# Attention front end of a fused kernel: transposes of F split, V projections ahead of P V, third g block in y's bank, finer weight slices

## Chip, cores, metric

One core of a Trainium2 chip. The metric is device microseconds of one execution, median over runs. The kernel before takes 568.84 us here (568.69 to 569.04, 4 runs).

## The reference, cut to what matters

```python
# attention with keys and values projected from 1024 to 64 rows, 8 batches x 8 heads, head size 64
k_proj = einsum('ks,bhsd->bhkd', E, k);  v_proj = einsum('ks,bhsd->bhkd', F, v)
attn   = softmax(q @ k_proj^T / 8);      x = attn @ v_proj          # -> x [8192, 512]
# gated feed-forward
out = (silu(x @ w_gate) * (x @ w_val)) @ w_out                      # 512 -> 1536 -> 512
```

The kernel cuts the 8192 tokens into 16 chunks of 512 and the 1536 hidden columns into 12 "features" of 128. For each chunk and feature there is a **g block** and a **v block** of four 128x128x512 matmuls. In the first chunk the first two features are done in half blocks of 256 tokens, as parts of x become ready.

## The kernel before

The change touches only what runs before the steady loop. The attention of the first chunk is done in four parts 0 to 3 (two head groups by two token halves): `u_S` scores and exp, `u_R` row sums, `u_N` normalization (on GpSimd; that of part 3 on DVE), `u_A` transposes of the normalized P, `u_PV*` P V product and its copy into xT, the feed-forward's input. Before and between them stand **warm-up matmuls** (`warm(n)`): n products of zeros whose result nobody reads.

```python
def u_V0(p0, p1, at):            # V projection of head pairs p0..p1, block diagonal in one bank
    t = bank(at, [P, p1 - p0, P], FP32, "kvp")
    nc.tensor.matmul(out=t, lhsT=zeros, rhs=zeros, start=True, stop=False)
    for j in range(NJ):
        for c in range(2):       # 16 matmuls; in the trace the two of a pair start 3 ns apart
            nc.tensor.matmul(out=t[64*c:64*c+64, :, 64*c:64*c+64], lhsT=FT[:, j, :], ...)
    nc.scalar.copy(out=BDV[0][:, p0:p1, :], in_=t[:])

def f_mm(c, f, w, i=None):       # one (half) block of g (w=0) or v (w=1)
    if i != 1:
        half[c, f, w] = bank("gv"[w], [P, CW], FP32, "gv"[w] + "ps")
    ...                          # four matmuls over wg or wv
# ... (cut) order of the front end in the kernel before, from part 3's scores on:
        u_S(0, 3, "v"); u_R(0, 3); u_A(0, 0, act); u_N(0, 3, dve)
        u_V0(0, 2, "y");  u_PV2(0, 0, 0, 0, act)
        u_V0(2, 3, "y");  u_A(0, 2, act)
        u_V0(3, 4, "v");  u_PV1(0, 0, 2, 0, dve)
        u_A(0, 1, dve);   u_PV1(0, 0, 3, 0, act)
        u_A(0, 3, act)
        load_w_gv(2, 4, (1,))
        f_mm(0, 0, 0, 0); u_PV2(0, 0, 0, 1, dve)
        f_mm(0, 0, 1, 0); f_mm(0, 1, 0, 0)
        u_PV2(0, 0, 1, 1, act); f_mm(0, 1, 1, 0)
```

The first dma calls of GpSimd are, in order: q, k, q, F, v (three parts), then g's weights of feature 0, v's of feature 0, g's of feature 1, v's of feature 1, and so on. `load_w_gv(c0, c1, which)` loads features c0 to c1 of g (0), v (1) or both.

The softmax here doesn't subtract the row's maximum and nothing guards it: scores larger than these inputs give would overflow.

## Time and profile before

| | before |
|---|---|
| time | 568.84 us |
| TensorE busy | 560.2 of 566.9 us |
| TensorE's waits for other engines, whole run | 3.0 us in 5 waits |
| first half block of the feed-forward starts | 20.70 us |
| third v block starts (dense from there on) | 25.93 us |

How to read it: TensorE is the bound from end to end, so a change to the front end can shift only the moment at which the dense stretch begins, as long as no later wait takes the lead back. That moment is the start of the third v block; the prediction shows the lines.

### The profile page before, as it was taken

Reading aid. Unit: us, or ns where it says so; the run is one execution under the profiler, and the core shown is the slowest. Engines: PE = TensorE matmul, PEld = TensorE weight load, DVE = VectorE, ACT = ScalarE, POOL = GpSimd, SP = SyncE. Lnnn points to the kernel's source line nnn. Section 1 sums busy time; section 2 is a strip of 40 time slices with the busy share of each in tenths; the row PEclk is TensorE's granted clock in tenths of the full one; section 3 lists DMA queues with packets and bytes.
Section 4 is the critical chain, followed back from the end, with each engine's and each line's share of the span. In section 5 each row is a group of like instructions: output and inputs, shape, how many; then the busy total and the mean of one; then the engine's idle time right before and its main releaser. Section 6 shows DMA issues by size and latency. Waiting matters only on the chain.

```text
span 566.9 us, 7938 instructions
## 1 busy us (share of the span) xinstructions
PE 560.2 (99%) x2970; PEld 266.3 (47%) x2970; DVE 339.2 (60%) x576; ACT 236.0 (42%) x417; POOL 110.4 (19%) x124
## 2 busy tenths in 40 slices
PE   8999999999999999999999999999999999999997
PEld 4654444444444444444444444444444444444444
DVE  3786664766476645766466655666547665545550
ACT  3664352444435433443434434354343543443222
POOL 6851250124012400124002230023100220000000
PEclk9999999999999999999999999999999999999999
DMA  9999989729913795029940499105990214100012
GB/s 201 194 200 188 175 126 199 141 57 187 192 50 74 113 196 119 38 57 163 183 83 37 76 185 204 38 19 101 200 183 20 57 38 75 38 37 32 25 38 93
DMA packets 111159, 62.78 MB, mean 111 GB/s; under 512 B 64272, under 2 KB 102416, under 8 KB 111120
## 3 DMA queue, kind: packets, MB, share of 16 engines
q0 software_dynamic: 42896, 29.49, 36.1%
q1 hardware_dynamic: 67392, 31.46, 26.2%
q10 hardware_dynamic: 832, 1.31, 0.8%
q8 instruction: 23, 0.38, 0.3%
q14 instruction: 16, 0.13, 0.1%
HBM read 60.29 MB, written 16.78 MB: 136 GB/s over the span
## 4 chain that ended last, share of the span: by engine, by line
PE 97%; ACT 1%; DVE 1%; issue 0%
PE gps L377 29%; PE yps L415 29%; PE vps L377 29%; PE kvp L150 3%; PE sc L271 2%; PE pv L328 2%; PE warm L513 1%; ACT ee L275 0%; ACT AT L138 0%; DVE BD L138 0%; ACT th L389 0%; PE qTp L237 0%; PE efp L501 0%; PE aTp L317 0%; PE pv L343 0%
## 5 line engine op out<-in xcount | busy, mean ns | idle before, releaser
L396 DVE SCALAR_TENSOR_TENSOR s<-th,gps 128x512 f32<-128x512 f32 x192 | 130.3, 679 | 134.4 <-ACT th L389 134.0
L377 PE MATMUL gps<-xT,wg 128*128 128x512 bf16 (+1 forms) x776 | 197.6, 377 | 0.1
L377 PE MATMUL vps<-xT,wv 128*128 128x512 bf16 (+1 forms) x776 | 197.5, 377 | 0.0
L415 PE MATMUL yps<-wo,hT 128*128 128x512 bf16 (+1 forms) x780 | 194.5, 376 | 0.0
L389 ACT ACTIVATE th<-gps 128x512 f32<-128x512 f32 x192 | 114.6, 597 | 159.0 <-PE gps L377 153.9
L401 DVE TENSOR_TENSOR hT<-s,vps 128x512 bf16<-128x512 f32 x192 | 131.9, 687 | 20.4 <-DVE s L396 0.5
L301 POOL TENSOR_TENSOR AAd<-ee,rr 128x512 bf16<-128x512 f32 x56 | 58.2, 1041 | 342.5 <-issue 180.6
L415 PEld LDWEIGHTS <-hT 128*128 128x128 bf16 x780 | 76.2, 98 | 89.9
L377 PEld LDWEIGHTS <-wv 128*128 128x128 bf16 x776 | 74.0, 98 | 83.3 <-issue 2.9
L377 PEld LDWEIGHTS <-wg 128*128 128x128 bf16 x776 | 74.0, 98 | 81.3 <-issue 1.2
L425 ACT ACTIVATE ysb<-yps 128x512 f32<-128x512 f32 (+1 forms) x65 | 38.4, 590 | 77.7 <-PE yps L415 77.7
L138 ACT CAST xT<-pv 128x512 bf16<-128x512 f32 (+1 forms) x62 | 35.9, 581 | 52.5 <-PE pv L328 50.3
L286 DVE TENSOR_REDUCE zz<-ee 128x8 f32<-128x512 f32 x64 | 43.4, 679 | 22.1 <-ACT ee L275 22.1
L275 ACT ACTIVATE ee<-sc 128x512 f32<-128x512 f32 x64 | 38.2, 597 | 19.8 <-PE sc L271 18.7
L271 PEld LDWEIGHTS <-qTd 128*128 128x128 bf16 x224 | 17.2, 98 | 13.2 <-DMA qTd<-qb 0.2
L328 PE MATMUL pv<-AT,BDV 128*128 128x512 bf16 x60 | 22.4, 379 | 0.1
L271 PE MATMUL sc<-BD,qTd 128*128 128x128 bf16 x224 | 21.6, 219 | 0.0
L288 DVE RECIPROCAL rr<-zz 128x8 f32<-128x8 f32 x64 | 13.0, 203 | 6.6 <-DVE zz L286 0.5
L108 POOL DMA_DIRECT2D qb<-in_q_dram x18 | 16.3, 907 | 1.4 <-POOLq L651 0.8
L150 PE MATMUL kvp<-kb,ET 128*64 128x512 bf16 (+1 forms) x72 | 15.5, 358 | 0.0
L162 DVE CAST BDV<-kvp 64x256 bf16<-64x256 f32 x7 | 3.0, 426 | 20.0 <-ACT ks L158 17.8
L150 PE MATMUL kvp<-vb,FT 128*64 128x512 bf16 x56 | 13.4, 382 | 0.0
(66 smaller groups left out, 137.6 us busy)
## 6 DMA issues: line engine op xcount, KB each, us to landing
out_dram<-ysb SPq DMA_DIRECT2D x63, 256.0 KB, 2.3
qb<-in_q_dram POOLq DMA_DIRECT2D x14, 512.0 KB, 18.1
kb<-in_k_dram POOLq DMA_DIRECT2D x7, 1024.0 KB, 11.0
vb<-in_v_dram POOLq DMA_DIRECT2D x7, 1024.0 KB, 14.5
wo<-in_moe_w_out_dram POOLq DMA_DIRECT2D x2, 768.0 KB, 21.9
wg<-in_moe_w_gate_dram POOLq DMA_DIRECT2D x5, 256.0 KB, 8.4
wv<-in_moe_w_val_dram POOLq DMA_DIRECT2D x5, 256.0 KB, 9.0
kraw<-in_k_dram ACTq DMA_DIRECT2D x2, 512.0 KB, 4.9
```

The costliest lines, as they stand in the source:

```text
L138: (nc.scalar.copy if eng is nc.scalar else eng.tensor_copy)(out=out, in_=in_)
L150: nc.tensor.matmul(out=t[lo : lo + 64, h0:h1].rearrange("p h d -> p (h d)"), lhsT=w[:, j, :], rhs=src[b][:, h0:h1, j, :], start=(j == 0), ...
L271: nc.tensor.matmul(out=ps[:, n, :], lhsT=t[:, n, :], rhs=BD[b % 2][:, 4 * g + n, :], start=True, stop=True)
L275: nc.scalar.activation(out=e[:].rearrange("p h j k -> p (h j k)"), in_=ps[:].rearrange("p a k -> p (a k)"), func=AF.Exp, scale=scale,)
L286: nc.vector.reduce_sum(out=z[:], in_=e[:], axis=AX.X)
L301: eng.tensor_tensor(out=a.rearrange("p j h k -> p h j k"), in0=ee.pop((b, u))[:], in1=rr.pop((b, u))[:].unsqueeze(3).to_broadcast([P, 4, 2 ...
L377: nc.tensor.matmul(out=ps[:, ts], lhsT=(wg, wv)[w][:, kt, f * P : (f + 1) * P], rhs=x[:, kt, ts], start=(kt == 0), stop=(kt == NKT - 1),)
L389: nc.scalar.activation(out=th[:], in_=ps[:], func=AF.Tanh, scale=0.5)
L396: nc.vector.scalar_tensor_tensor(out=s1[:], in0=th[:], scalar=1.0, in1=g[:], op0=ALU.add, op1=ALU.mult)
L401: nc.vector.tensor_tensor(out=hT[c][:, f, :], in0=s1[:], in1=ps[:], op=ALU.mult)
L415: nc.tensor.matmul(out=yy[c][:, cs], lhsT=hT[c][:, f, i * P : (i + 1) * P], rhs=wo[:, f, cs], start=(f == 0), stop=(f == NFT - 1),)
L425: nc.scalar.activation(out=ysb[:, cs], in_=yy[c][:, cs], func=AF.Copy, scale=0.5)
```

## The change

Its intent: start the feed-forward earlier. F is transposed earlier and its copies are shared between DVE and ACT; V of the first two head pairs is projected in a wide form (8 matmuls instead of 17); the first g half block stands ahead of the transposes of P parts 1 and 3; the third g block borrows y's bank; the normalization of part 3 moves from DVE to GpSimd; the weights come in slices of 1, 1, 1, 2, 2, 2, 2, 1 features.

```diff
+    def u_V0w(p0, p1, at):          # 8 matmuls of 256 columns into partitions 64..127, two ACT copies
...
-            half[c, f, w] = bank("gv"[w], [P, CW], FP32, "gv"[w] + "ps")
+            where = "y" if (c, f, w) == (0, 2, 0) else "gv"[w]
+            half[c, f, w] = bank(where, [P, CW], FP32, where + "ps")
...
-        load_w_gv(2, 4, (0,))
+        load_w_gv(2, 3)
...
-        warm(1)
+        turn(1, "a", (0,), dve)
...
+        turn(1, "a", (1,))
         u_S(0, 2, "g")
...
-        turn(1, "a", (0,))
+        load_w_gv(3, 5, (0,))
...
-        turn(1, "a", (1,))
         u_S(0, 3, "v")
         u_R(0, 3)
+        u_N(0, 3)
+        load_w_gv(3, 5, (1,))
         u_A(0, 0, act)
-        u_N(0, 3, dve)
-        u_V0(0, 2, "y")
+        u_V0w(0, 2, "y")
+        u_V0(2, 3, "v")
         u_PV2(0, 0, 0, 0, act)
-        u_V0(2, 3, "y")
-        u_A(0, 2, act)
-        u_V0(3, 4, "v")
+        u_A(0, 2, dve)
+        u_V0(3, 4, "y")
         u_PV1(0, 0, 2, 0, dve)
+        u_PV1(0, 0, 3, 0, act)
+        f_mm(0, 0, 0, 0)
         u_A(0, 1, dve)
-        u_PV1(0, 0, 3, 0, act)
+        f_mm(0, 0, 1, 0)
+        u_PV2(0, 0, 0, 1, dve)
         u_A(0, 3, act)
-        load_w_gv(2, 4, (1,))
-        f_mm(0, 0, 0, 0)
-        u_PV2(0, 0, 0, 1, dve)
-        f_mm(0, 0, 1, 0)
         f_mm(0, 1, 0, 0)
         u_PV2(0, 0, 1, 1, act)
         f_mm(0, 1, 1, 0)
...                                  # later slices: (5,7), q, q, (7,9), (9,11), (11,12)
```

More of the change, by code (lines that the diff above doesn't have):

```diff
@@ L185, in u_V0 @@
         nc.scalar.copy(out=BDV[0][:, p0:p1, :], in_=t[:])
+    def u_V0w(p0, p1, at):
+        t = bank(at, [P, p1 - p0, 2, D], FP32, "kvp")
+        for j in range(NJ):
+            nc.tensor.matmul(
+                out=t[64:P].rearrange("p a c d -> p (a c) d"),
+                lhsT=FT[:, j, :],
+                rhs=vb[0][:, 2 * p0 : 2 * p1, j, :],
+                start=(j == 0),
+                stop=(j == NJ - 1),
+            )
+        for c in range(2):
+            rows = slice(64 * c, 64 * c + 64)
+            nc.scalar.copy(out=BDV[0][rows, p0:p1, rows], in_=t[64:P, :, c, :])
     def u_KT(b, at="a", prs=(0, NPAIR)):
@@ L495, with turn @@
         nc.vector.memset(ks[0][64:P], 0.0)
-        def turn(which, at, halves=(0, 1)):
+        nc.vector.memset(BDV[0][:, 0:2], 0.0)
+        def turn(which, at, halves=(0, 1), eng=nc.scalar):
             for half in halves:
@@ L506, in turn @@
                 js = slice(4 * half, 4 * half + 4)
-                copy(nc.scalar, (ET, FT)[which][:, js, :], ps[:])
+                copy(eng, (ET, FT)[which][:, js, :], ps[:])
         def warm(n):
@@ L581 @@
         nc.vector.memset(BDV[1][:], 0.0)
-        load_w_gv(4, 6)
+        load_w_gv(5, 7)
         load_q(0, 1, hs=(0, 4))
-        load_w_gv(6, 8)
         load_q(0, 1, hs=(4, 8))
-        load_w_gv(8, 10)
-        load_w_gv(10, 12)
+        load_w_gv(7, 9)
+        load_w_gv(9, 11)
+        load_w_gv(11, 12)
         load_q(1, 0)
```

## The prediction

> **What bounds the kernel now.** I read four views, in this order: the page, who waited for whom on TensorE, the timeline of TensorE over the first 75 us, and the landing times of single transfers. The page first. Columns of its first line: busy us, share of the span, number of instructions.
>
> ```profile
> PE 560.2 (99%) x2970; PEld 266.3 (47%) x2970; DVE 339.2 (60%) x576; ACT 236.0 (42%) x417; POOL 110.4 (19%) x124
> PE   8999999999999999999999999999999999999997
> PEclk9999999999999999999999999999999999999999
> ```
>
> TensorE is busy from end to end at the full clock. Nothing in the diff touches a tile after feature 2 of the first chunk of tokens except the order of loads, so all gain and all loss lie in the first 25 us or so. The waits of TensorE in the whole run (us in total, times, longest) say how little can be had there:
>
> ```profile
> PE sc L271 <- DVE BD L138: 0.7, 1, 0.7
> PE pv L343 <- ACT BDV L185: 0.7, 1, 0.7
> PE pv L355 <- ACT AT L138: 0.2, 1, 0.2
> PE aTp L317 <- DVE xT L138: 0.2, 1, 0.2
> ```
>
> The last three, 1.1 us, are in the stretch that is rearranged. The timeline (start us, duration us, what; L377 is the feed-forward, L178 the V projection, L343 the P V product, L317 a transpose of P) shows where that stretch ends:
>
> ```profile
> 17.88 0.39 PE L343 MATMUL pv<-AT,BDV 128*128 128x256 bf16 x2 [0.68 <-ACT BDV L185]
> ...
> 20.48 0.38 PE L317 MATMUL aTp<-ident_bf,AA 128*128 128x128 bf16 x4 [0.18 <-DVE xT L138]
> 20.70 0.60 PE L377 MATMUL gps<-xT,wg 128*128 128x256 bf16 x4
> ...
> 21.36 0.60 PE L377 MATMUL vps<-xT,wv 128*128 128x256 bf16 x4
> ...
> 22.45 0.60 PE L377 MATMUL vps<-xT,wv 128*128 128x256 bf16 x4
> 22.89 0.78 PE L377 MATMUL gps<-xT,wg 128*128 128x256 bf16 x4
> 23.50 0.60 PE L377 MATMUL vps<-xT,wv 128*128 128x256 bf16 x4
> ...
> 25.07 1.02 PE L377 MATMUL gps<-xT,wg 128*128 128x512 bf16 x4
> 25.93 1.03 PE L377 MATMUL vps<-xT,wv 128*128 128x512 bf16 x4
> ```
>
> The starts tell what the durations hide. A half block of four 256-column matmuls is followed 0.44 us later by the next, a whole block of 512 columns 0.86 us later. Two starts are late: after 22.89 comes 23.50 (0.61, so 0.17 lost: that block waits midway for the last xT, which ACT finishes at 23.24), and the last half block at 24.38 is followed at 25.07 and not at 24.82 (0.25 lost: the third g waits for a g bank, which DVE frees at 25.02). From 25.93 on the starts are dense, 0.86 us apart, with 0.45 us of gaps in all up to 75 us. So **the number to predict is the start of the third v block (feature 2), 25.93 us**; whatever that moves by, the end moves by.
>
> The landings matter because the weights come just in time. The first half of v's weights for feature 0, issued at 8.65, has this line:
>
> ```profile
> DMA to landing us min/median/max: 12.5/12.5/12.5
> ```
>
> It lands at 21.18, 0.18 us before its use at 21.36. Read the same way: g of feature 0 lands at 18.84, g of feature 1 at 21.36 (used 21.80), v of feature 1 at 21.95 (used 22.45), the pair 2-3 at 23.29 and 24.65.
>
> **What the Trainium skill says.** "PSUM — Partial Sum Buffer", Specifications, gives 8 banks per partition; the pools take 2 (g), 2 (v), 1 (y) and 3 (attention), so the third g can only wait or borrow y's. The trace agrees (the 0.25 us). "DMA: Bandwidth & Descriptors", section Why a DMA increments its semaphore by 16 and not by 1: all 16 engines post one and only the full count means landed. The trace shows what that costs: of the sixteen increments for v of feature 0, fifteen came by 19.58 and the last at 21.18. "Runtime: NRT & Kernel Launch", Terms: instruction memory is refilled in 16 KiB blocks. In the trace's packets a 16,384-byte one of the instruction queue starts at 19.15 and holds one DMA engine for 0.945 us; that is the late sixteenth. "GPSIMD Engine Reference", Engine selection, calls a two-input elementwise operation on GpSimd some 2 times slower than on VectorE; here it does not hold: the normalization took 1.04 us on POOL and 1.13 on DVE.
>
> **The change part by part.** I replayed the new order by hand, with durations from this trace and about 0.04 to 0.1 us from one engine's end to the next one's start.
>
> *F's turns.* F lands at 13.11; its first four transposes (0.44 us) take the place of one warm matmul (0.39 us), whose time was a wait for ks (ACT, to 13.57) anyway. Cost 0. One FT copy goes to DVE, the other stays on ACT but ahead of the exps. Exp 0.60 and FT copy 0.38 had alternated (starts 14.94, 15.68, 16.42); now the exps follow each other at 0.49: about 15.01, 15.50, 15.99. The last exp is 0.43 us earlier, and with it the copy of the first transposed P (16.91 to 16.48).
>
> *V ahead.* The wide form does 8 matmuls of 256 columns (0.109 each, 0.87 us) for 16 of 128 that ran two at a time (0.42 us from first to last start) and a zeroing: TensorE about 0.25 us more, while it waits anyway. Its result is ready at 16.9, two copies of some 0.27 end at 17.5; V of pair 2, gated by its data (16.88), fills TensorE until about 17.15. The first P V starts at 17.55 instead of 17.88. The transposes of P part 2 follow at 17.85 (18.63 before), V of pair 3 at 18.2 (data 18.11), the two small P V products at 18.7 and 19.0, and the copies of xT end at 19.7. The first g half block then starts at 19.1, waits for these copies, and ends about 19.9: **some 1.2 us earlier than before** (21.14).
>
> *What follows it.* The order is now transposes of P part 1 (20.1), v of feature 0, P V, transposes of part 3, g of feature 1, P V, v of feature 1, then the second halves. Part 3 is normalized on POOL behind two weight issues (0.75 each): ready near 20.6. From the transposes of part 3 a chain runs that TensorE cannot cover: to ACT's copy 0.42, copy 0.59, P V, 0.42 to its copy, 0.59, the second half of a g block. From the start of v's half block of feature 0 to the v block that stood at 23.50 this makes 0.65 + 1.07 + 1.06 + 0.22, about 3.0 us; before, the transposes of part 3 came ahead of everything. So that block starts at (landing of v of feature 0) + 3.06. **Break-even is a landing at 20.45.** If the data is there at 20.1, the P V ahead of it waits for DVE's copy and the block starts at 23.35: gain 0.15.
>
> *Third g in y's bank.* It removes the 0.25 us, but the v block behind needs v's first bank, freed by tanh 0.60, DVE 0.69 and 0.69: about 2.37 us after the block of 23.50, where it was 2.43. Gain 0.06, not 0.25.
>
> *Slices.* Same bytes. The stretch of small slices moved 178 to 186 GB/s against 196 in the two-feature ones, so four more small transfers of 128 KB cost 4 x 0.05 = 0.2 us of queue. With them feature 3 lands at about 24.7 (g) and 26.05 (v), its uses stand at 26.80 and 27.66; the second chunk's q lands at 30.05 and 31.4, uses 31.98 and 34.37; the last w_out at 57.3, use 59.41. All hidden.
>
> Sum if v of feature 0 is early: -0.15 - 0.06 = -0.2 us. If it lands at 21.18 as now: 21.18 + 3.06 = 24.24 against 23.50, +0.74 - 0.06 = +0.7 us.
>
> **Rivals.** *(1) The instruction fetch moves behind the transfer.* TensorE's stream is about 20 instructions shorter up to here, so the same instruction count is reached later in the work; if the fetch starts after 19.3, v of feature 0 lands at 19.6 and the time is 568.7. *(2) The fetch stays or comes slightly earlier*, since TensorE reaches that work sooner: the landing stays between 20.3 and 21.2, TensorE idles up to 1.1 us at the first v half block and the time is 568.9 to 569.6. For it: no load ahead of that transfer changes. *(3) The gain of 1.2 us at the first g carries through*: 567.7. Against it: g and v of feature 1 land at 21.36 and 21.95, which caps the start of the second halves near 22.5 instead of 22.89 even if all else is free. *(4) A later wait eats it all*: POOL now makes parts 1 and 3 between weight issues; were it 1 us later than I have it, 569.5. The trace speaks against, since no issue there would wait for a semaphore.
>
> **Range and chances.** I give the early landing (568.7) somewhat over half, the late one (569.3 to 569.6) a third, the rest to (3). The centre is 568.8. The range 568.1 to 569.7 spans all but the far ends. Two per cent is 11.4 us, ten times the whole of TensorE's waits here: same is all but certain.
>
> **What would show it.** Right: first P V near 17.55, first g half block done near 19.9, no wait before the third g, later starts dense from the third v block. The deciding reading is the start of the first v half block and what ended the wait before it: a landing of wv before 20.5 means a gain of 0.1 to 0.2, one near 21.2 a loss. Wrong: a third v block before 25.3, or a new wait for weights after 26 us.

## The result, and the profile after

568.57 us (568.5 to 568.64, 4 runs) against 568.84 us; ratio 0.9995, 95% interval 0.9978 to 1.0012. Ratios here are the mean time of one kernel's fast runs over that of the other's of the same rounds, so not quite the ratio of the medians quoted.

TensorE's line of the page, and its waits (us in total, times, longest), of the changed kernel:

```profile
PE 560.3 (99%) x2960; PEld 266.2 (47%) x2960; DVE 339.2 (60%) x578; ACT 235.7 (42%) x416; POOL 113.0 (20%) x127
```

```profile
PE sc L286 <- DVE BD L138: 0.7, 1, 0.7
PE efp L520 <- DMA Eraw<-in_E_dram: 0.4, 1, 0.4
PE pv L358 <- ACT BDV L200: 0.3, 1, 0.3
PE pv L358 <- ACT AT L138: 0.2, 1, 0.2
```

The wait for the first P V is down from 0.7 to 0.3 us, the one ahead of the last transposes is gone, and the 0.2 us for ACT's copy of transposes (`AT`) now stand in front of the last P V product, in the middle of the feed-forward's half blocks. The wait for E lies ahead of all edited work on TensorE. The timeline of TensorE in the changed kernel, same stretch (L395 feed-forward, L358 P V, L332 transposes):

```profile
17.68 0.39 PE L358 MATMUL pv<-AT,BDV 128*128 128x256 bf16 x2 [0.26 <-ACT BDV L200]
...
19.20 0.89 PE L395 MATMUL gps<-xT,wg 128*128 128x256 bf16 x4
...
20.16 0.60 PE L395 MATMUL vps<-xT,wv 128*128 128x256 bf16 x4
20.83 0.38 PE L358 MATMUL pv<-AT,BDV 128*128 128x256 bf16 x2
21.05 0.39 PE L332 MATMUL aTp<-ident_bf,AA 128*128 128x128 bf16 x4
...
22.11 0.38 PE L358 MATMUL pv<-AT,BDV 128*128 128x256 bf16 x2 [0.24 <-ACT AT L138]
...
23.38 0.60 PE L395 MATMUL vps<-xT,wv 128*128 128x256 bf16 x4
...
24.69 1.03 PE L395 MATMUL yps<-xT,wg 128*128 128x512 bf16 x4
25.74 1.02 PE L395 MATMUL vps<-xT,wv 128*128 128x512 bf16 x4
```

The first g half block starts 1.5 us earlier (20.70 to 19.20) and the first v half block 1.2 us (21.36 to 20.16), but the v block that stood at 23.50 stands at 23.38 and the third v at 25.74 instead of 25.93. The gain shrinks between 20.83 and 23.38: transposes of part 3 at 21.05, their copy on ACT (21.47 to 22.06), P V at 22.11, its copy (22.52 to 23.11), second half of the g block. That is the chain that the prediction named. And 0.07 of the 0.19 us are not the change's: the first scores, ahead of any edited instruction but one memset in DVE's idle time, already start at 10.83 instead of 10.90. Such a shift differs from run to run: in the two later profiles of the same kernel they start at 10.62 and 10.60. v of feature 0 landed early (issued at 8.55; at 19.47):

```profile
DMA to landing us min/median/max: 10.9/10.9/10.9
```

### The profile page after: what moved, and what is told of

Read it like the earlier page. It is cut to its first block, busy times and chain, and to the rows that moved or that the text cites. A ratio compares the mean times of both kernels' runs of the same rounds, so it can differ in the third digit from the quotient of the medians.

```text
span 566.8 us, 7925 instructions
## 1 busy us (share of the span) xinstructions
PE 560.3 (99%) x2960; PEld 266.2 (47%) x2960; DVE 339.2 (60%) x578; ACT 235.7 (42%) x416; POOL 113.0 (20%) x127
## 4 chain that ended last, share of the span: by engine, by line
PE 97%; ACT 1%; DMA 1%; DVE 0%; issue 0%; POOL 0%
PE yps L433 29%; PE vps L395 29%; PE gps L395 29%; PE kvp L150 3%; PE sc L286 2%; PE pv L343 2%; DMA Eraw<-in_E_dram 1%; ACT ee L290 0%; PE qTp L252 0%; PE aTp L332 0%; PE warm L532 0%; PE efp L520 0%; PE pv L358 0%; ACT AT L138 0%; POOL AA L316 0%
## 5 line engine op out<-in xcount | busy, mean ns | idle before, releaser
L395 PE MATMUL vps<-xT,wv 128*128 128x512 bf16 (+1 forms) x776 | 197.5, 377 | 0.0
L395 PE MATMUL gps<-xT,wg 128*128 128x512 bf16 (+1 forms) x772 | 196.9, 377 | 0.0
L395 PEld LDWEIGHTS <-wv 128*128 128x128 bf16 x776 | 73.9, 98 | 83.5 <-issue 3.2
L395 PEld LDWEIGHTS <-wg 128*128 128x128 bf16 x776 | 74.0, 98 | 80.9 <-issue 0.8
```

Source lines behind the costliest of these rows:

```text
L395: nc.tensor.matmul(out=ps[:, ts], lhsT=(wg, wv)[w][:, kt, f * P : (f + 1) * P], rhs=x[:, kt, ts], start=(kt == 0), stop=(kt == NKT - 1),)
```

## The experiments

All times are against the kernel before on the same chip (568.73 to 568.77 us median in each set). "Early" and "late" below mean the landing of feature 0's v weights. The landing is known only for the one profiled run of each set; the others are called early or late by their times. Each interval is some 0.25% (1.4 us) wide, so differences of a few tenths rest on single profiles and on how runs group.

### 1. The changed kernel again, twice

No edit. 

> The changed kernel as it is, for a closer interval and a second profile. Theory A (the change works by an earlier first feed-forward block; what it gains is bounded by the chain from the transposes of P part 3, and 0.07 of the 0.19 us seen at the third v block were there before the change begins to act, at the first scores): 0.1 to 0.3 us under the kernel before, third v block at 25.7 to 25.8. Rival B (the landing of the first v weights is luck: this profile caught it early at 19.47 us, others catch it late at 21.2): some runs or this profile show the third v block at 26.4 or later and times near 569.3.

Measured: 569.10, 569.14, 569.29, 569.18 and 568.48 us; ratio 1.0005 (0.9992 to 1.0017). **Four of the five are slower than the kernel before.** The profile, of the run with 569.10, shows why (landing of v of feature 0; below it TensorE's timeline):

```profile
DMA to landing us min/median/max: 12.3/12.3/12.3
```

```profile
20.94 0.61 PE L395 MATMUL vps<-xT,wv 128*128 128x256 bf16 x4 [0.83 <-DMA wv<-in_moe_w_val_dram]
...
23.94 0.60 PE L395 MATMUL vps<-xT,wv 128*128 128x256 bf16 x4
...
26.30 1.02 PE L395 MATMUL vps<-xT,wv 128*128 128x512 bf16 x4
```

Issued at 8.55, the weights landed at 20.90 (fifteen of sixteen increments by 19.30). The v block behind the chain stands at 23.94 = 20.90 + 3.04; the third v at 26.30. Rival B of the expectation holds: the same program has early and late runs.

The last set had the changed kernel once more. 

> The changed kernel once more, on the chip of the three runs above: a mixture of early runs (568.4 to 568.7) and late ones (569.1 to 569.3); in the profile, fetch after the first increment of v of feature 0 and landing near 19.5, or fetch before it and landing near 20.9.

Measured: 569.05, 568.50, 568.57, 568.67, 568.46; ratio 0.9998 (0.9985 to 1.0010). The profiled run is the late one: landing 20.86, third v 26.26. Over the 14 runs of the changed kernel nine are early, by their times, with a mean of 568.55 us and five late with a mean of 569.15; together 568.77, which is what the kernel before takes. The four runs of the first result were all early.

### 2. The third g in g's own bank

```diff
-            where = "y" if (c, f, w) == (0, 2, 0) else "gv"[w]
+            where = "gv"[w]
```

> The changed kernel with the third g block in g's own bank again. Theory A: the third v block behind it waits for v's bank anyway, so only about 0.06 us is lost: third g late by 0.2 to 0.25, third v at 25.80 to 25.85, time 0.05 to 0.1 us above the changed kernel. Rival C (borrowing y's bank is what gained the 0.27 us): 0.2 to 0.3 us above the changed kernel, third v near 26.0.

Measured: 568.63, 568.60, 568.55, 568.48 and a late 569.17 us. The early mean, 568.57, is that of the changed kernel. Timeline:

```profile
23.40 0.60 PE L395 MATMUL vps<-xT,wv 128*128 128x256 bf16 x4
...
24.97 1.02 PE L395 MATMUL gps<-xT,wg 128*128 128x512 bf16 x4
25.84 1.03 PE L395 MATMUL vps<-xT,wv 128*128 128x512 bf16 x4
```

The third g is 0.26 us later behind the block at 23.40, the third v only 0.08 (2.44 against 2.36). Here the third v follows the third g directly (0.87 us); in the changed kernel it starts 1.05 us behind it, 0.19 us more than the 0.86 of two dense blocks, as v's bank is not free yet. So all but 0.08 us of the early third g is lost again. Rival C falls.

### 3. Feature 0's v weights late on purpose

```diff
-        load_w_gv(0, 1)
+        load_w_gv(0, 1, (0,))
         load_w_gv(1, 2, (0,))
+        load_w_gv(0, 1, (1,))
```

> The changed kernel with feature 0's v weights loaded behind feature 1's g weights, so that they land late on purpose (about 21.2 where 19.47 was). Theory A: the transposes of P part 3 stand behind the first v half block, so everything moves: first v half block at about 21.2, the v block that stood at 23.38 at landing + 3.06 = 24.2, third v at 26.6, time 0.8 to 0.9 us above the changed kernel. Rival D (the later weights set the pace, feature 1's land late anyway): the third v block moves by less than 0.3 us.

Measured: 569.37 us (569.30 to 569.39), 0.8 above the early runs of the changed kernel. Landing 21.18, first v half block 21.22, then:

```profile
24.22 0.60 PE L395 MATMUL vps<-xT,wv 128*128 128x256 bf16 x4
```

24.22 = 21.18 + 3.04, third v 26.58. Rival D falls. One landing makes the difference, and with it always late there are no early runs.

### 4. More instructions ahead

```diff
-            for _ in range(n):   # each rhs=zeros[:] (512 columns)
+            for _ in range(2 * n):   # each rhs=zeros[:, 0:256]
```

> The changed kernel with every warm-up matmul of 512 columns cut in two of 256: same time on TensorE, 17 more matmuls (34 more instructions) ahead of everything. Theory A: the fetch of 16,384 bytes at 19.12 us is TensorE's instruction stream and comes at an instruction count, so it comes earlier, at 17.5 to 18.7 us, and holds one of the sixteen increments of the first g or v weights: v of feature 0 complete at 19.9 to 21.2 instead of 19.47, third v block 0 to 0.8 us later. Rival E (the fetch comes at a time, or belongs to another engine): fetch at 19.1 as now and no change in landings or time.

Measured: 569.64 us (569.49 to 570.65). The 16,384-byte packet starts at 17.03 instead of 19.12. The DMA view counts it, between 19 and 20 us in the changed kernel and between 17 and 18 us here (queue, kind, packets, MB, share of 16 engines):

```profile
q8 instruction: 1, 0.02, 5.9%
```

```profile
q8 instruction: 1, 0.02, 5.6%
```

It now holds the last part of the raw v, whose last increment comes at 19.21, 1.2 us behind the fifteenth (17.98):

```profile
19.25 0.44 PE L178 MATMUL kvp<-vb,FT 128*64 128x64 bf16 x16 [0.84 <-DMA vb<-in_v_dram]
```

The third v stands at 26.70. So the packet is moved by TensorE's instruction stream, not bound to a moment, and the transfer that ends while it is moved lands late. So do those behind it: the last increments of g and v of feature 0 came at 19.66 and 20.40, 0.96 and 0.97 us behind their fifteenth. The expectation had named these two as what would bind; it was the raw v, and the loss at the third v (0.96 us) is above the 0 to 0.8 expected. One of the five runs, 570.65, stands alone; its granted clock was 0.997, that of the others 0.999 or 1.0.

### 5. The slices of before

The changed kernel with the loads of before: `load_w_gv(2, 4, (0,))` in place of `(2, 3)`, `load_w_gv(2, 4, (1,))` behind the three normalizations, then (4,6), q, (6,8), q, (8,10), (10,12).

> The changed kernel with the weight slices and the order of loads of the kernel before. Theory A: the new slices are hidden, so this changes nothing by itself: early runs at 568.5 to 568.6, late ones at 569.1 to 569.3, third g and v at the same distance (1.31 and 2.36 us) behind the v block of the second halves of feature 0. Rival F (the single slice of feature 2 lands just in time and is part of the gain): a wait for wg or wv before the third g or v block, third v later by over 0.2 us.

Measured: 568.52 us (568.50 to 568.91); third v at 25.73. No effect on the time, as theory A has it. But there is a hidden one: in this kernel, which has no weight issue between the three normalizations, the transfers fall to some 160 GB/s between 22 and 26 us, and the transposed q of batch 1 lands at 60.52 instead of 59.75. Its first use stands at 61.00, so 0.5 us of slack hid it. The next runs met it.

### 6. Part 3 first, and the whole chain early

First run: both weight issues behind the three normalizations, and

```diff
         u_A(0, 1, dve)
+        u_A(0, 3, act)
         f_mm(0, 0, 1, 0)
         u_PV2(0, 0, 0, 1, dve)
-        u_A(0, 3, act)
-        f_mm(0, 1, 0, 0)
         u_PV2(0, 0, 1, 1, act)
+        f_mm(0, 1, 0, 0)
         f_mm(0, 1, 1, 0)
```

> The changed kernel with the two normalizations of parts 1 and 3 on GpSimd ahead of the weight issue between them, and the transposes of part 3 ahead of the first v half block, both P V products behind it. Theory A (the chain from these transposes sets the second halves): where v of feature 0 lands early (19.5), the v block that stood at 23.38 starts near 22.8, the third v at 25.1 and the time is near 568.0; where it lands late (20.9), the third v stands near 25.5 and the time is near 568.3. Rival D (the landing of feature 1's weights, 21.2 and 21.5, sets the second halves): gain under 0.2 us, 568.4 or more.

Measured: 567.91 to 569.81, median 568.40 (6 runs). The profiled run is late (landing 20.93, 568.66 us): block behind the chain at 23.16 and third v at 25.52, where the changed kernel's late run has 23.94 and 26.30:

```profile
23.16 0.60 PE L395 MATMUL vps<-xT,wv 128*128 128x256 bf16 x4
...
25.52 1.02 PE L395 MATMUL vps<-xT,wv 128*128 128x512 bf16 x4
```

So the chain from part 3's transposes is what sets these starts, and rival D falls at the third v. But only 0.4 us of the 0.8 reach the end. The six runs do not form two groups, and the longest, 569.81 us at a granted clock of 1.0, is not explained.

Second run: as the first; besides, `u_A(0, 1)` between the two small P V products, `u_A(0, 3)` right behind the first g half block, the P V product of part 1 ahead of the first v half block, and the third v in a bank of the attention pool (`"ya"[w] if (c, f) == (0, 2)`).

> As the run with part 3 first, and the transposes of part 1 between the two small P V products, those of part 3 right behind the first g half block, and the third v block in a bank of the attention pool besides the third g in y's. Theory A: v block of the second halves of feature 0 near 22.55, third v directly behind third g, near 24.75, and about 567.6 in early runs; 25.3 and 568.2 in late ones. If the third v still waits (for DVE, not for a bank) or for its weights, the gain over the run with part 3 first is under 0.15 us.

Measured: 568.52 us median (567.74 to 568.66). Third v at 24.92, 0.8 us ahead of the changed kernel, in an early run, but the time of that run, 568.52, is the changed kernel's. Where it went (timeline, TensorE's waits for transfers after 26 us):

```profile
35.33 1.04 PE L395 MATMUL vps<-xT,wv 128*128 128x512 bf16 x4 [0.28 <-DMA wv<-in_moe_w_val_dram]
...
60.98 0.40 PE L286 MATMUL sc<-BD,qTd 128*128 128x128 bf16 x4 [0.24 <-DMA qTd<-qb]
```

It hit two landings that had been hidden: v's weights of feature 7 took 0.4 us of the lead, the transposed q of batch 1 (60.93) the rest; the scores start at 60.98, in the changed kernel at 61.00. The transfers themselves were slower. Stretches of 2 us, last column GB/s; first this run, then the changed kernel:

```profile
24.00:26.00 2.00, 1.95 (x12) 0.93 (x11) 1.79 (x4) 1.01 (x2) 2.00 (x4) 1.00 1.30 155
26.00:28.00 2.00, 2.00 (x11) 0.94 (x10) 1.90 (x4) 0.60 (x1) 1.23 (x2) 1.00 1.35 170
```

```profile
24.00:26.00 2.00, 1.98 (x14) 1.14 (x13) 1.69 (x3) 1.02 (x3) 2.00 (x4) 1.00 1.40 187
26.00:28.00 2.00, 2.00 (x11) 0.92 (x10) 1.79 (x4) 0.69 (x2) 2.00 (x3) 1.00 1.44 195
```

All three kernels with 3.8 us or more between two starts of weight issue (this one, the one before it, experiment 5) show it; the kernel before, with 3.6 us, and the changed one, with 2.8, do not or hardly; single 512-byte packets, 60 ns as a rule, then took up to 1.2 us (experiment 5). The length of that pause was never changed alone: the slices, their order and the place of the issue changed with it. So that the pause slows the transfers is a guess from these profiles, and what a packet waits for was not tested.

### 7. TensorE's order alone

The loads and GpSimd's order as in the changed kernel; only

```diff
-            where = "y" if (c, f, w) == (0, 2, 0) else "gv"[w]
+            where = "ya"[w] if (c, f) == (0, 2) else "gv"[w]
...
         u_A(0, 1, dve)
+        u_A(0, 3, act)
         f_mm(0, 0, 1, 0)
         u_PV2(0, 0, 0, 1, dve)
-        u_A(0, 3, act)
```

> The changed kernel with the loads and GpSimd's order as they are; only TensorE's order and a bank differ: the transposes of part 3 stand ahead of the first v half block, and the third v block borrows a bank of the attention pool. What the two runs before it gained at the third v block (0.7 to 0.8 us) they lost by 61 us, where the transposed q of the second batch lands at 60.9 to 61.1 instead of 59.75, because the weight issue held back behind GpSimd's normalizations let the transfers fall to 140 to 177 GB/s between 22 and 28 us. Theory A with this addition: transfers as in the changed kernel, transposed q at 59.6 to 59.8, third v at 25.1 to 25.2 where v of feature 0 lands early and 25.5 where late; 567.9 to 568.1 in early runs, 568.2 to 568.4 in late ones. If the gain is lost again with the transposed q at 59.75, another wait behind 26 us takes it.

Measured: 568.20 us (568.04 to 568.43); ratio to the kernel before 0.9990 (0.9977 to 1.0002). In the profiled run, an early one (568.04):

```profile
20.46 0.40 PE L332 MATMUL aTp<-ident_bf,AA 128*128 128x128 bf16 x4 [0.34 <-POOL AA L316]
20.70 0.60 PE L395 MATMUL vps<-xT,wv 128*128 128x256 bf16 x4
...
24.37 1.03 PE L395 MATMUL gps<-xT,wg 128*128 128x512 bf16 x4
25.23 1.03 PE L395 MATMUL vps<-xT,wv 128*128 128x512 bf16 x4
```

The third v follows the third g without a gap, now that it has a bank of its own, and stands 0.51 us ahead of the changed kernel's early run; the end, too, comes 0.51 us earlier (566.26 against 566.77), and the transposed q lands at 59.44. Of the 0.51 us 0.2 are an early start (first P V at 17.48 instead of 17.68). Counted from the first P V, the v block of feature 0's second halves comes 0.12 us sooner (5.58 against 5.70 us) and the third v 0.31 us (7.75 against 8.06): in an early run the borrowed bank brings 0.19 us and the moved transposes 0.12, since these now wait 0.34 us for GpSimd's normalization of part 3. The mean of the five runs, 568.21, is 0.34 under the changed kernel's early ones. No run is above 568.43, as expected if late data finds the transposes that start the chain already done; no late run was profiled here, so that is not shown. By the mean this is the best version, ahead of both kernels in every one of its five runs but by one part in a thousand, and its interval against the kernel before just includes 1.

### 8. Moving the fetch later: three misses

Changed kernel without the last three warm-up matmuls: 

> The changed kernel without its last three warm-up matmuls (the single one and the pair), which stand in waits: TensorE reaches every later instruction 6 instructions sooner in count, so by theory A the fetch of its instruction stream comes 0.2 to 0.6 us later than 18.9 to 19.1, behind the last of v of feature 0's packets; all five runs then are early, 568.4 to 568.6. Rival B' (early or late is decided by something else, as the moment of the first loads): both kinds of runs again, with the fetch where it was. If the clock falls[...], the record of the clock shows it and the run says nothing.

Measured: 569.00, 569.03, 569.07, 568.38, 568.22 us; in the profile, a late one, fetch at 18.75, landing 20.83. Both kinds of runs again; a miss.

Changed kernel with the second warm-up group cut from 4 to 1 (`warm(4)` to `warm(1)`): 

> The changed kernel with the second group of warm-up matmuls cut from 4 to 1. The run that dropped three later ones (at 9.7 and 11.5 us) did not move the fetch later; the one that added 34 instructions before 8 us moved it 2.1 us earlier. If what starts the fetch is an instruction count reached before 9.7 us, 6 instructions fewer at 7 to 8 us move it 0.2 to 0.6 us later, to 19.2 to 19.7, behind v of feature 0's packets (first increment 18.9 to 19.1): all runs early, 568.4 to 568.7. If the fetch does not follow the count: 18.7 to 19.15 again and both kinds of runs, as before.

Measured: 568.98 to 569.31 us, all late; fetch at 18.73, landing 20.76. A miss: against the changed kernel's late profiles (fetch at 18.87 and 18.78, first feed-forward block at 19.00 and 18.97) fetch and block (18.93) have hardly moved, and not later. That all five are late is not explained.

That edit with the order of experiment 7: 

> Both edits together. If both hold: all runs early, third v near 25.15, 567.9 to 568.1, better than the kernel before by 0.7 us.

Measured: 568.12 to 568.18 in four runs and 569.15 in one; fetch at 19.01, landing 19.51, third v at 25.33. The fetch edit adds nothing to experiment 7. The one long run was not profiled: a late landing alone should have cost less, by experiment 7's expectation. Its granted clock was 0.997, that of the other four 1.0; 0.3% of the span is up to 1.7 us, so the clock may well be the cause.

## Why the prediction was right, point by point

- **Bound and place.** Right: TensorE's busy time is 560.3 us (560.2 before), and beyond the third v block the starts are dense in both kernels.
- **F's turns and V ahead.** Right in mechanism, by the timeline; no run undid either part alone. First P V at 17.68, predicted 17.55. The mis-sized term is the start of ACT's two copies of V: taken as 16.97, they started at 17.09 (ACT was copying P's transposes until 17.07) and ended at 17.63, not 17.5. Behind the first g half block the next work starts at 19.94, predicted 19.9.
- **Chain of 3.06 us behind the landing of v of feature 0.** Right, and the best tested step: 3.04 in experiments 1 and 3. (Its four terms sum to 3.00; the 0.06 left is the time from landing to start, which measured 0.04.) In the early case 23.38, predicted 23.35.
- **Third g in y's bank.** 0.06 us predicted, 0.08 measured (experiment 2). That the third g "can only wait or borrow y's" was too narrow a view of the banks: in experiment 7 the attention pool had one to lend, to the third v, and the wait behind the third g was gone.
- **Slices.** Hidden, as predicted; feature 3's landed at 24.28 (g) and 25.62 (v), some 0.4 us sooner than foretold. What the prediction did not see is that the three kernels without a weight issue between the three normalizations moved their weights more slowly (experiments 5 and 6) and the changed one did not; that was hidden too, and only a faster front end feels it.
- **Early or late.** That the landing decides was right, and the two outcomes of rivals 1 and 2 are both seen, run by run, of one program. But the early landing of the first result did not come about as rival 1 said: the fetch did not move behind the transfer, it stood at 19.12 (19.14 before); the transfer came earlier, with its first increment at 18.88 instead of 19.20, and got ahead of the fetch. So that part was luck, and so were four early runs of four. "Somewhat over half" early was 9 of 14. The 568.7 foretold for early runs was 568.55, of which 0.07 us is a start that had nothing to do with the change. For late runs 569.3 to 569.6 was said and 569.15 measured, since these landings came at 20.86 and 20.90, not 21.18.
- **Rival 3** (the whole 1.2 us carries through) is wrong for this order of work: with the early landing the chain still held the third v at 25.74.
- **GpSimd against VectorE.** The prediction's "here it does not hold" is not shown. The one normalization on DVE (18.10 to 19.23) ran beside one on GpSimd until 18.68, so its 1.13 us may hold a wait; no run has it alone.
- **Still open.** What starts the fetch. Adding 34 instructions moved it 2.1 us earlier, taking away 6 did not move it later. A fixed count it is not: by the traces 285 to 292 weight loads and matmuls of TensorE had started before it with the usual warm-up, 280 to 283 with 6 fewer and 242 with 34 more (some records may be missing). In twelve of the thirteen profiles of changed and edited kernels it starts 0.04 to 0.25 us ahead of the first feed-forward block (in experiment 4, 3.1 us). Late runs have it 0.18 us or more ahead of the first increment of the transfer that it delays, early ones between 0.10 ahead and 0.24 behind. This orders the profiles of the changed kernel and its edits; the kernel before, late with 0.06 ahead, does not fit, and no run set the lead on purpose toward the early side. That a few tenths at the start of a run decide is thus a guess.

## What to carry to other kernels

When a front end is pulled forward under a bound engine, follow the longest chain of copies that starts behind the moved work: here 1.2 us gained at the first block became 0.1 us three copies later, until the transposes that start the chain were moved ahead of the wait (0.8 us at the v block behind the chain in the late profile of experiment 6, 0.1 in the early one of experiment 7). Work that needs no late data should stand ahead of a just-in-time landing, since in an in-order queue everything behind it inherits its jitter. And four equal runs can all be of one kind: the next set of runs of the same program showed the other.

## What the Trainium skill lacked or had wrong

- "Runtime: NRT & Kernel Launch", Instruction fetch mechanics, has the next 16 KiB block fetched while the current one is executed, and calls the cost of crossing a block's end "mostly hidden". Here a packet of 16,384 bytes took 0.89 to 0.95 us, the last of sixteen increments of a weight load came up to 1.6 us after the fifteenth (19.58 to 21.18, 19.30 to 20.90), and late runs are 0.6 us longer than early ones.
- "DMA: Bandwidth & Descriptors", Specifications, puts the size for line rate at 512 bytes or more. Slices with 256-byte rows moved 178 to 186 GB/s, those with 512-byte rows 195 to 198 (the kernel before, 18 to 31 us). The page is not contradicted, but the loss here is under a tenth.
- No page has it that a pause of some 4 us between two starts in the issue of software-generated transfers may slow those that follow: 155 to 180 GB/s for 6 us instead of 187 to 196 (experiment 6; the pause was not changed alone).
- "GPSIMD Engine Reference", Engine selection, has a two-input elementwise operation some 2 times slower than on VectorE; a 128x512 float32 product with a broadcast operand and bf16 output took 1.04 us on GpSimd and 1.13 on VectorE. The page is not shown wrong by it, since that one run on VectorE overlapped one on GpSimd by 0.58 us.
